# A rational activation's denominator moved from VectorE to ScalarE and Pool, in a fused delta rule and feed-forward kernel

## The chip, the cores and the metric

The kernel runs on one core of a Trainium2 chip. A core has a matrix engine (TensorE; PE in the profile, with its weight loads as PEld), VectorE (DVE), ScalarE (ACT), Pool (GpSimd) and SyncE (SP, which here only issues DMAs). Each engine takes its own instructions in order. The metric is the device time of one execution in microseconds; the median of three runs of the kernel before is 764.67 us (763.59 to 764.72).

## What is computed

A delta-rule attention over 4 batches, 8 heads, 768 steps and a head size of 48 (with the keys divided by their norms), and on its output a feed-forward part with a rational activation:

```python
for t in range(S):
    y[t] = q[t] @ state
    state = state + beta[t] * outer(k[t], v[t] - k[t] @ state)
x = y, heads side by side               # 3072 tokens x 384
h = x @ w_in                            # 3072 x 2048
P = a[0] + a[1]*h + a[2]*h**2 + a[3]*h**3
Q = 1 + abs(b[0])*abs(h) + abs(b[1])*h**2
out = (P / (Q + 1e-6)) @ w_out          # 3072 x 384
```

## The kernel before

Time is cut into 12 chunks of 64 steps. For each chunk the delta rule is solved in matrix form (stages keys, gram, inverse, blocks, solve, next, outputs), with two f16 halves for each operand and so three matmul passes for each product. A chunk yields 256 tokens, all batches side by side. The feed-forward part handles them in 8 units of 256 hidden columns each, 96 units in all. A unit's tile is 128 partitions x 512 (two blocks of 128 hidden columns, 256 tokens each).

One unit n runs through these steps:

- `hidden` (L857): 18 matmuls of 256 columns into `ph`, a PSUM tile of the pool `ps_h` (two buffers).
- `numerator` (L874): ScalarE makes z = |B1 ph| (L884) and u = A3 ph + a2 (L885). VectorE makes w = (z + B0) ph (L888), ScalarE w = |w| (L890). B1, B0, A3 and the like are columns of a small table `msc`, one number for each partition. w, u and z lie in an SBUF tile `mx` with three buffers.
- `cubic` (L892): VectorE multiplies u by ph (L896) and makes (u + A1) ph (L898).
- `quotient` (L900): ScalarE makes ln(w + Q0) (L904) and exp of its negative (L906), the reciprocal of the denominator. VectorE makes the f16 result `mg` (L910), and with two more products the remainder for its lower half (L913, which writes into the next unit's `ph`, and L915). Pool multiplies that remainder by the reciprocal (L917) into the second half of `mg`.
- `accumulate` (L919): 12 matmuls of 384 columns (L931) with both halves into `po`; after the last unit of a chunk the sum is scaled (L948) and stored.

The delta rule's small steps use the same engines: casts on ScalarE (L207, L215), their remainders on VectorE (L217) or Pool (L213), scaling of keys on Pool (L501).

Nothing is scheduled at run time. Every step is a generator that issues a few instructions for each `next`, and a table of numbers, `PLACES`, holds for each step of each chunk or unit its place in the whole program's order; `run` sorts by it and calls them one after the other. That sets the order on every engine, and the tile pools add the waits. By that table the hidden steps of 88 of the 96 units come before the last chunk's tokens are made, before the change and after it.

## Time and profile before

| | before |
|---|---|
| median of three runs | 764.67 us |
| the profiled execution | 765.28 us |
| its span, first to last instruction | 763.6 us |
| VectorE busy | 691.9 us |
| ScalarE busy | 661.1 us |
| TensorE busy | 629.3 us |
| Pool busy | 311.7 us |

The span is what the profile shows; 1.7 us of the execution lie outside it. Busy time of an engine counts the time in which at least one of its instructions is under way, so the durations of neighbours that overlap add up to more than it. Ends of matmuls are modelled. Shares are of the span.

### The profile page before, as it was taken

To read this page: it belongs to the slowest core of one execution; us is meant where nothing else is said; L and a number is where in the kernel's file an instruction comes from. 1 tells how busy PE (TensorE), PEld (TensorE's weight loads), DVE (VectorE), ACT (ScalarE), POOL (GpSimd) and SP (SyncE) were. 2 spreads that over 40 slices of the span, in tenths; PEclk is the share of its full clock that TensorE was granted. 3 is DMA by queue.
4 is the path that set the end of the run, shared out by engine and by line. 5 is a ranking of instruction groups with operands and counts; after the bars stand their busy time and mean duration, and the time that the engine had idled before them with its cause. 6 is when DMAs were issued, how large, how long until landed. Compare 5 with 4: busy or idle time off the path is not lost.

```text
span 763.6 us, 23465 instructions
## 1 busy us (share of the span) xinstructions
PE 629.3 (82%) x9520; PEld 506.6 (66%) x9520; DVE 691.9 (91%) x1288; ACT 661.1 (87%) x1301; POOL 311.7 (41%) x321
## 2 busy tenths in 40 slices
PE   1321455886898999898998999999989999999986
PEld 1221455675677788686776787787778877777753
DVE  6789988867898999898998999999989999999995
ACT  4685998978898999798997999999989996899883
POOL 6742262533344265154342463354542432323222
PEclk9955786999799999899999999999999999999999
DMA  9699999778737675678464777685755832600000
GB/s 215 194 213 196 191 174 149 119 130 129 134 73 124 88 117 98 109 124 127 89 115 81 131 118 119 108 131 87 139 81 103 138 58 36 109 1 23 1 21 22
DMA packets 358412, 84.35 MB, mean 110 GB/s; under 512 B 349856, under 2 KB 352928, under 8 KB 358304
## 3 DMA queue, kind: packets, MB, share of 16 engines
q1 hardware_dynamic: 356128, 81.69, 61.0%
q8 instruction: 75, 1.23, 0.7%
q10 hardware_dynamic: 2176, 1.17, 0.5%
q14 instruction: 33, 0.27, 0.1%
HBM read 34.70 MB, written 13.65 MB: 63 GB/s over the span
## 4 chain that ended last, share of the span: by engine, by line
DVE 32%; ACT 25%; PE 20%; DMA 10%; issue 5%; SPq 3%; POOL 2%; ACTq 0%; DVEq 0%; POOLq 0%
PE ph L864 7%; PE po L931 5%; DVE mx L888 3%; ACT mx L885 3%; DVE ph L913 3%; ACT mx L884 3%; DVE mx L915 3%; DVE mx L896 3%; DVE mg L910 3%; DVE mx L898 3%; ACT kp L815 2%; DVE w_out L311 2%; PE pu L396 2%; ACT mx L904 2%; ACT mx L890 2%
## 5 line engine op out<-in xcount | busy, mean ns | idle before, releaser
L917 POOL TENSOR_TENSOR mg<-mx 128x512 f16<-128x512 f32 x96 | 129.7, 1351 | 277.2 <-DVE mx L915 167.5
L931 PE MATMUL po<-w_out,mg 128*128 128x384 f16 x1152 | 214.5, 329 | 4.3 <-POOL mg L917 2.4
L864 PE MATMUL ph<-xT,w_in 128*128 128x256 f16 x1728 | 205.1, 273 | 10.9 <-DVE mx L915 9.3
L864 PEld LDWEIGHTS <-w_in 128*128 128x128 f16 x1728 | 165.6, 98 | 41.0 <-DVE mx L915 9.3
L931 PEld LDWEIGHTS <-mg 128*128 128x128 f16 x1152 | 109.5, 99 | 65.8 <-POOL mg L917 3.1
L910 DVE SCALAR_TENSOR_TENSOR mg<-mx,msc 128x512 f16<-128x512 f32 x96 | 73.3, 764 | 2.7 <-ACT mx L906 2.6
L884 ACT ACTIVATE mx<-ph,msc 128x512 f32<-128x512 f32 x96 | 65.2, 679 | 12.0 <-PE ph L864 10.1
L913 DVE SCALAR_TENSOR_TENSOR ph<-mx,msc,mg 128x512 f32<-128x512 f32 x96 | 73.7, 768 | 1.5
L885 ACT ACTIVATE mx<-ph,coef,msc 128x512 f32<-128x512 f32 x96 | 74.1, 772 | 0.0
L888 DVE SCALAR_TENSOR_TENSOR mx<-mx,msc,ph 128x512 f32<-128x512 f32 x96 | 70.7, 737 | 1.9 <-issue 1.1
L915 DVE SCALAR_TENSOR_TENSOR mx<-mx,msc,ph 128x512 f32<-128x512 f32 x96 | 71.1, 741 | 1.3
L898 DVE SCALAR_TENSOR_TENSOR mx<-mx,msc,ph 128x512 f32<-128x512 f32 x96 | 70.8, 738 | 0.7
L904 ACT ACTIVATE mx<-mx,msc 128x512 f32<-128x512 f32 x96 | 69.3, 722 | 1.1
L890 ACT ACTIVATE mx<-mx 128x512 f32<-128x512 f32 x96 | 60.3, 628 | 10.7 <-DVE mx L888 10.4
L396 PEld LDWEIGHTS <-kbd 128*128 128x128 f16 x1680 | 57.6, 102 | 16.9 <-DVE sw L328 7.3
L896 DVE TENSOR_TENSOR mx<-ph,mx 128x512 f32<-128x512 f32 x96 | 65.4, 681 | 0.4 <-issue 0.2
L396 PEld LDWEIGHTS <-ebd 128*128 128x128 f16 x1728 | 51.2, 98 | 15.6 <-issue 11.4
L396 PE MATMUL pu<-z,ebd 128*128 128x48 f16 x1728 | 52.0, 186 | 11.4 <-DVE z L217 10.1
L906 ACT ACTIVATE mx<-mx 128x512 f32<-128x512 f32 x96 | 60.1, 628 | 1.1
L396 PEld LDWEIGHTS <-wbd 128*128 128x128 f16 x1152 | 33.2, 98 | 40.4 <-issue 38.7
L213 POOL TENSOR_TENSOR mm<-m,mm 128x512 f16<-128x512 f32 x24 | 31.6, 1328 | 34.4 <-ACT mm L207 28.1
L217 DVE SCALAR_TENSOR_TENSOR z<-pu,zmask,z 128x768 f16<-128x768 f32 x36 | 36.4, 1011 | 5.7 <-ACT z L215 5.7
(196 smaller groups left out, 1194.0 us busy)
## 6 DMA issues: line engine op xcount, KB each, us to landing
wsi<-in_moe_w_in_dram SPq DMA_DIRECT2D x8, 768.0 KB, 6.5
wso<-in_moe_w_out_dram SPq DMA_DIRECT2D x8, 768.0 KB, 6.5
gd<-g SPq DMA_DIRECT2D x24, 256.0 KB, 4.6
mbd<-mm SPq DMA_DIRECT2D x24, 256.0 KB, 5.3
wc<-img SPq DMA_DIRECT2D x24, 256.0 KB, 5.1
...
```

The costliest lines, as they stand in the source:

```text
L396: nc.tensor.matmul(dst[p][:, h], head(bd, lp, p * H + h), head(rt, rp, p * H + h), start=start and n == 0 and h == 0, stop=stop and n == l ...
L864: nc.tensor.matmul(ph[:, i], w_in[:, f2, wp, cc, i * P : (i + 1) * P], x[:, xp, cc], start=k == 0, stop=k == 3 * NCC - 1,)
L884: nc.scalar.activation(z, ph, AF.Abs, scale=B1)
L885: nc.scalar.activation(u, ph, AF.Identity, scale=A3, bias=a2)
L888: nc.vector.scalar_tensor_tensor(out=w, in0=z, scalar=B0, in1=ph, op0=ALU.add, op1=ALU.mult)
L896: nc.vector.tensor_mul(u, ph, u)
L898: nc.vector.scalar_tensor_tensor(out=u, in0=u, scalar=A1, in1=ph, op0=ALU.add, op1=ALU.mult)
L910: nc.vector.scalar_tensor_tensor(out=g[:, 0], in0=u, scalar=A0, in1=r, op0=ALU.add, op1=ALU.mult)
L913: nc.vector.scalar_tensor_tensor(out=t, in0=w, scalar=Q0, in1=g[:, 0], op0=ALU.add, op1=ALU.mult)
L915: nc.vector.scalar_tensor_tensor(out=u, in0=u, scalar=A0, in1=t, op0=ALU.add, op1=ALU.subtract)
L917: nc.gpsimd.tensor_mul(g[:, 1], u, r)
L931: nc.tensor.matmul(po[p], g[:, gp, i, p * P : (p + 1) * P], w_out[:, f2, wp, i], start=f2 == lo and i == 0 and k == 0, stop=f2 == hi - 1 a ...
```

## The change

The denominator |b1| h^2 + |b0| |h| is now made from the absolute value alone. ScalarE makes z = |ph| with the constant scale 1 and w = B1 z + B0, with a column as scale and a column as bias; Pool makes w = w z. VectorE has no step in it. `POOL_UNITS` names the units of a chunk for which this holds: all eight. Three more edits go with it: `numerator` stops after z, so that u has a place of its own; `hidden` stops between its two blocks of nine matmuls; and the norm sums of the weights' tables (two matmul calls) go to the buffers of `ps_h` instead of `ps_f`. The table `PLACES` is new throughout, with 3188 places where there were 2996.

```diff
     def total(src, n, nm, pool=ps_f, tag="a"):
-        pf = pool.tile([P, NPAIR * 512 if pool is ps_f else n], F32, tag=tag, name="pf" + nm)[:, :n]
+        pf = pool.tile([P, NPAIR * 512 if pool is ps_f else TG], F32, tag=tag, name="pf" + nm)[:, :n]
...
+    POOL_UNITS = (0, 1, 2, 3, 4, 5, 6, 7)
...
-        pt = total(io, hi - lo, f"o{lo}", ps_f, "a")
+        pt = total(io, hi - lo, f"o{lo}", ps_h, "h")
...
         ph = ps_h.tile([P, 2, TG], F32, tag="h", name=f"ph_{n}")
+        unit[n] = {"ph": ph}
         for i in range(2):
...
-        unit[n] = {"ph": ph}
+            if i == 0:
+                yield
...
-        nc.scalar.activation(z, ph, AF.Abs, scale=B1)
+        on_pool = f2 in POOL_UNITS
+        nc.scalar.activation(z, ph, AF.Abs, scale=1.0 if on_pool else col(1))
+        yield
+        A3, B1, _, B0, A0, Q0 = (col(i) for i in range(6))
         nc.scalar.activation(u, ph, AF.Identity, scale=A3, bias=a2)
         d.update(u=u, w=w, r=r, A0=A0, Q0=Q0)
         yield
-        nc.vector.scalar_tensor_tensor(out=w, in0=z, scalar=B0, in1=ph, op0=ALU.add, op1=ALU.mult)
-        yield
-        nc.scalar.activation(w, w, AF.Abs)
+        if on_pool:
+            nc.scalar.activation(w, z, AF.Identity, scale=B1, bias=B0)
+            yield
+            nc.gpsimd.tensor_mul(w, w, z)
+        else:
+            nc.vector.scalar_tensor_tensor(out=w, in0=z, scalar=B0, in1=ph, op0=ALU.add, op1=ALU.mult)
+            yield
+            nc.scalar.activation(w, w, AF.Abs)
...
     PLACES = {
         "hidden": (
-            (439,),
+            (395, 436),
...
```

ScalarE's order around unit 29 (the sixth of chunk 3), whose tile is `mx_6136`, in the kernel before, from its absolute value of `ph` to its second absolute value; `mx_6012` and `mx_6248` are the units ahead of and behind it, `z_1` is a step of the delta rule's solve:

```order
L904 ACTIVATE mx_6012<-mx_6012,msc_5451 128x512
L884 ACTIVATE mx_6136<-ph_6117,msc_5451 128x512 [waits PE_49,Pool_49]
L885 ACTIVATE mx_6136<-ph_6117,coef,msc_5451 128x512
L215 ACTIVATE z_1_6191<-pu_6058,zmask 128x768 [waits DVE_49,PE_49,Pool_49]
L906 ACTIVATE mx_6012<-mx_6012 128x512 [waits Activation_49]
L225 ACTIVATE sq_7_6208,fs_6207<-v_6139 128x768 [waits DMAHW7_49,DMAHW0_49]
L890 ACTIVATE mx_6136<-mx_6136 128x512 [waits DVE_49]
L884 ACTIVATE mx_6248<-ph_6229,msc_5451 128x512 [waits PE_49,Pool_49]
```

The same engine and unit now, its tile is `mx_6026`, from the absolute value (L889) over u (L892) and the affine step (L896) to the logarithm (L916); L918 is the exponential, `xT` the tokens' halves, `lgx` a scale's logarithm:

```order
L889 ACTIVATE mx_6026<-ph_5996 128x512 [waits PE_49]
L242 ACTIVATE lgx_6033<-xs_5934 128x1 [waits DVE_49]
L243 ACTIVATE lgx_6033<-lgx_6033,consts 128x1 [waits Activation_49]
L892 ACTIVATE mx_6026<-ph_5996,coef,msc_5343 128x512
L896 ACTIVATE mx_6026<-mx_6026,msc_5343 128x512
L553 COPY wt_92<-bblk 128x16
L215 ACTIVATE xT_5933<-px_6014,sf_5935 128x768 [waits DVE_49,PE_49]
L918 ACTIVATE mx_5931<-mx_5931 128x512
L215 ACTIVATE z_0_6137<-pu_6073,zmask 128x768 [waits PE_49]
L916 ACTIVATE mx_6026<-mx_6026,msc_5343 128x512 [waits Pool_49]
```

Where ScalarE waited for VectorE ahead of the second absolute value, it now waits for Pool ahead of the logarithm, and four instructions of other work lie between the affine step and that wait.

Pool's order in the kernel before, with the remainders' products of units 25 to 27 (`mg_5788`, `mg_6018`, `mg_6055`); `kw` is the scaling of the keys, `kn`, `rr` and `mm` are remainders of the delta rule:

```order
L501 TENSOR_TENSOR kw<-kw,nrm_5650 128x16x48 [waits DMAHW6_49,DMAHW5_49,DMAHW7_49,DMAHW4_49,DVE_49]
L917 TENSOR_TENSOR mg_5788<-mx_5631 128x512 [waits DVE_49,PE_49]
L213 TENSOR_TENSOR rr_5992<-v_3786,rr_5992 128x384 [waits Activation_49]
L917 TENSOR_TENSOR mg_6018<-mx_5717 128x512 [waits DVE_49,PE_49]
L213 TENSOR_TENSOR kn_90<-kw,kn_90 128x2x2x48 [waits Activation_49,Pool_49]
L213 TENSOR_TENSOR kn_90<-kw,kn_90 128x2x2x48
L213 TENSOR_TENSOR rr_5992<-v_3786,rr_5992 128x384
L213 TENSOR_TENSOR mm_6034<-m_6_6027,mm_6034 128x4x2x64 [waits DMAHW1_49,DMAHW0_49,Activation_49]
L213 TENSOR_TENSOR mm_6034<-m_6_6027,mm_6034 128x4x2x64
```

Pool's order now, at the same units: L929 are the remainders' products of units 25 to 27 (`mg_5773`, `mg_5860`, `mg_6029`), L898 with `mx_5931` and `mx_6026` the denominators of units 28 and 29, L502 the scaling of the keys:

```order
L929 TENSOR_TENSOR mg_5773<-mx_5494 128x512 [waits DVE_49,PE_49]
L502 TENSOR_TENSOR kw<-kw,nrm_5478 128x16x48 [waits DMAHW3_49,DMAHW2_49,DMAHW4_49,DMAHW1_49,DVE_49]
L929 TENSOR_TENSOR mg_5860<-mx_5606 128x512 [waits DVE_49,PE_49,Activation_49]
L898 TENSOR_TENSOR mx_5931<-mx_5931 128x512 [waits Activation_49,Pool_49]
L213 TENSOR_TENSOR rr_6009<-v_3920,rr_6009 128x384 [waits Activation_49]
L213 TENSOR_TENSOR kn_90<-kw,kn_90 128x2x2x48 [waits DMAHW6_49,DMAHW5_49,Pool_49]
L213 TENSOR_TENSOR rr_6009<-v_3920,rr_6009 128x384
L898 TENSOR_TENSOR mx_6026<-mx_6026 128x512 [waits Activation_49,Pool_49]
L213 TENSOR_TENSOR kn_90<-kw,kn_90 128x2x2x48
L929 TENSOR_TENSOR mg_6029<-mx_5748 128x512 [waits DVE_49,PE_49]
L213 TENSOR_TENSOR mm_6192<-m_6_6006,mm_6192 128x4x2x64 [waits DMAHW2_49,DMAHW1_49,Activation_49]
```

Two denominators stand between what was there, each behind Pool instructions that wait for other engines.

The last rows of ScalarE in the kernel before, from the second absolute value of unit 94 (`mx_13742`) on; unit 95 is `mx_13775`, L948 the scaling of the result:

```order
L890 ACTIVATE mx_13742<-mx_13742 128x512 [waits DVE_49]
L884 ACTIVATE mx_13775<-ph_13752,msc_13461 128x512 [waits PE_49,Pool_49]
L885 ACTIVATE mx_13775<-ph_13752,coef,msc_13461 128x512
L904 ACTIVATE mx_13742<-mx_13742,msc_13461 128x512 [waits Activation_49]
L906 ACTIVATE mx_13742<-mx_13742 128x512 [waits Activation_49]
L890 ACTIVATE mx_13775<-mx_13775 128x512 [waits DVE_49]
L904 ACTIVATE mx_13775<-mx_13775,msc_13461 128x512 [waits Activation_49]
L906 ACTIVATE mx_13775<-mx_13775 128x512 [waits Activation_49]
L948 ACTIVATE ob_13860<-po_0_0_13612,kp_0_13264 128x384 [waits DMAHW7_49,DMAHW6_49,PE_49]
L948 ACTIVATE ob_13860<-po_0_1_13613,kp_0_13264 128x384 [waits PE_49]
```

The same place now, with units 94 (`mx_13744`) and 95 (`mx_13778`):

```order
L889 ACTIVATE mx_13744<-ph_13725 128x512 [waits PE_49,Pool_49]
L892 ACTIVATE mx_13744<-ph_13725,coef,msc_13477 128x512
L896 ACTIVATE mx_13744<-mx_13744,msc_13477 128x512 [waits Activation_49]
L889 ACTIVATE mx_13778<-ph_13759 128x512 [waits PE_49,Pool_49]
L892 ACTIVATE mx_13778<-ph_13759,coef,msc_13477 128x512
L896 ACTIVATE mx_13778<-mx_13778,msc_13477 128x512 [waits Activation_49]
L916 ACTIVATE mx_13744<-mx_13744,msc_13477 128x512 [waits Pool_49]
L918 ACTIVATE mx_13744<-mx_13744 128x512 [waits Activation_49]
L916 ACTIVATE mx_13778<-mx_13778,msc_13477 128x512 [waits Pool_49]
L918 ACTIVATE mx_13778<-mx_13778 128x512 [waits Activation_49]
L960 ACTIVATE ob_13860<-po_0_0_13616,kp_0_13299 128x384 [waits DMAHW7_49,DMAHW6_49,PE_49]
L960 ACTIVATE ob_13860<-po_0_1_13617,kp_0_13299 128x384 [waits PE_49]
```

ScalarE now makes z, u and w of both units first, and then the logarithms and exponentials, each logarithm behind a wait for Pool.

## Rows read from the trace of the kernel before

**Rows 1.** The page's busy line: busy us of each engine, share of the span, number of instructions.

```profile
PE 629.3 (82%) x9520; PEld 506.6 (66%) x9520; DVE 691.9 (91%) x1288; ACT 661.1 (87%) x1301; POOL 311.7 (41%) x321
```

**Rows 2.** Busy time of each engine in three stretches that make up the span. The columns are the stretch and its length in us, then busy us (instructions) of PE, PEld, DVE, ACT and POOL, the granted TensorE clock, the DMA engines' share and GB/s.

```profile
0.00:180.00 180.00, 86.75 (x1494) 73.30 (x1495) 146.35 (x294) 139.94 (x286) 86.55 (x107) 0.81 0.88 174
180.00:660.00 480.00, 450.06 (x7115) 365.57 (x7114) 451.93 (x845) 439.64 (x864) 195.62 (x192) 0.98 0.64 106
660.00:764.00 104.00, 92.50 (x915) 67.77 (x912) 93.62 (x152) 81.55 (x153) 29.57 (x24) 0.99 0.11 22
```

**Rows 3.** The same view for four shorter stretches.

```profile
420.00:480.00 60.00, 59.08 (x946) 47.93 (x945) 59.06 (x111) 58.35 (x116) 28.20 (x29) 1.00 0.73 122
480.00:540.00 60.00, 58.40 (x945) 47.82 (x943) 58.53 (x108) 58.01 (x114) 27.57 (x27) 1.00 0.66 106
660.00:750.00 90.00, 86.09 (x878) 64.33 (x876) 88.86 (x146) 79.27 (x150) 26.60 (x22) 1.00 0.10 21
750.00:764.00 14.00, 6.40 (x39) 3.44 (x36) 4.76 (x7) 2.28 (x4) 2.97 (x2) 0.96 0.11 29
```

**Rows 4.** Groups of instructions by line and shape: instructions of a unit on VectorE, ScalarE and Pool. After the bar: busy us, mean ns of one, idle us of the engine just before them and what ended most of it.

```profile
L917 POOL TENSOR_TENSOR mg<-mx 128x512 f16<-128x512 f32 x96 | 129.7, 1351 | 277.2 <-DVE mx L915 167.5 <-ACT mx L904 18.4 <-PE pu L396 10.5
...
L885 ACT ACTIVATE mx<-ph,coef,msc 128x512 f32<-128x512 f32 x96 | 74.1, 772 | 0.0
...
L910 DVE SCALAR_TENSOR_TENSOR mg<-mx,msc 128x512 f16<-128x512 f32 x96 | 73.3, 764 | 2.7 <-ACT mx L906 2.6
...
L888 DVE SCALAR_TENSOR_TENSOR mx<-mx,msc,ph 128x512 f32<-128x512 f32 x96 | 70.7, 737 | 1.9 <-issue 1.1 <-ACT mx L885 0.7
L904 ACT ACTIVATE mx<-mx,msc 128x512 f32<-128x512 f32 x96 | 69.3, 722 | 1.1
L896 DVE TENSOR_TENSOR mx<-ph,mx 128x512 f32<-128x512 f32 x96 | 65.4, 681 | 0.4 <-issue 0.2
L884 ACT ACTIVATE mx<-ph,msc 128x512 f32<-128x512 f32 x96 | 65.2, 679 | 12.0 <-PE ph L864 10.1 <-DVE msc L847 0.7 <-DVE mg L910 0.5
L890 ACT ACTIVATE mx<-mx 128x512 f32<-128x512 f32 x96 | 60.3, 628 | 10.7 <-DVE mx L888 10.4
L906 ACT ACTIVATE mx<-mx 128x512 f32<-128x512 f32 x96 | 60.1, 628 | 1.1
```

**Rows 5.** The timeline of one unit near the end, where only the feed-forward part runs: start us, duration us, engine, line and operation; in brackets the idle time before it. L864 is the hidden step, L931 the second matmul.

```profile
740.10 2.14 PE L864 MATMUL ph<-xT,w_in 128*128 128x256 f16 x18
...
742.08 2.11 PE L931 MATMUL po<-w_out,mg 128*128 128x384 f16 x12
...
742.74 0.76 DVE L913 SCALAR_TENSOR_TENSOR ph<-mx,msc,mg 128x512 f32<-128x512 f32 x1
...
743.54 0.75 DVE L915 SCALAR_TENSOR_TENSOR mx<-mx,msc,ph 128x512 f32<-128x512 f32 x1
...
744.20 0.74 DVE L888 SCALAR_TENSOR_TENSOR mx<-mx,msc,ph 128x512 f32<-128x512 f32 x1
...
744.34 2.14 PE L864 MATMUL ph<-xT,w_in 128*128 128x256 f16 x18
744.45 1.28 POOL L917 TENSOR_TENSOR mg<-mx 128x512 f16<-128x512 f32 x1 [2.95 <-ACT mx L904]
744.86 0.68 DVE L896 TENSOR_TENSOR mx<-ph,mx 128x512 f32<-128x512 f32 x1
...
745.46 0.82 DVE L910 SCALAR_TENSOR_TENSOR mg<-mx,msc 128x512 f16<-128x512 f32 x1
746.21 0.73 DVE L898 SCALAR_TENSOR_TENSOR mx<-mx,msc,ph 128x512 f32<-128x512 f32 x1
...
746.98 0.76 DVE L913 SCALAR_TENSOR_TENSOR ph<-mx,msc,mg 128x512 f32<-128x512 f32 x1
```

**Rows 6.** The first view again, for line 888 alone: busy us and number of its instructions in two of the three stretches.

```profile
0.00:180.00 180.00, 2.97 (x4) 0.81 0.88 174
180.00:660.00 480.00, 52.98 (x72) 0.98 0.64 106
```

**Rows 7.** Two groups of casts from PSUM on ScalarE, the first with a column as scale, the second with a constant.

```profile
L215 ACT ACTIVATE z<-pu,zmask 128x768 f16<-128x768 f32 x36 | 32.3, 897 | 7.8 <-PE pu L396 7.8
...
L215 ACT ACTIVATE et<-pe 128x768 f16<-128x768 f32 x12 | 9.7, 805 | 1.7 <-PE pe L396 1.7
```

**Rows 8.** The timeline in the middle of the span: a product on Pool that starts while VectorE is in L910.

```profile
442.23 0.75 DVE L910 SCALAR_TENSOR_TENSOR mg<-mx,msc 128x512 f16<-128x512 f32 x1
...
442.48 1.63 POOL L917 TENSOR_TENSOR mg<-mx 128x512 f16<-128x512 f32 x1 [2.96 <-ACT mx L885]
```

**Rows 9.** Who waited for whom: us in total, times, longest us.

```profile
ACT mx L890 <- DVE mx L888: 10.4, 15, 2.0
...
ACT mx L884 <- PE ph L864: 10.1, 17, 3.2
...
PE ph L864 <- DVE mx L915: 9.3, 13, 2.0
...
ACT z L215 <- PE pu L396: 7.8, 8, 2.6
```

More of the change, by code (lines that the diff above doesn't have):

```diff
@@ L877, in numerator, with col @@
         d = unit[n]
-        A3, B1, A1, B0, A0, Q0 = (toks[c]["m"][:, i, f2 : f2 + 1] for i in range(6))
+        def col(i):
+            return toks[c]["m"][:, i, f2 : f2 + 1]
         ph = d["ph"]
@@ new lines @@
+            (54,),
+            (150,),
+            (524,),
+            (710,),
+            (928,),
+            (1178,),
+            (1420,),
+            (1682,),
+            (1905,),
+            (2173,),
+            (2442,),
+        ),
+        "load_q": (
+            (26,),
+            (147,),
+            (373,),
+            (526,),
+            (655,),
+            (910,),
+            (1210,),
+            (1408,),
+            (1704,),
+            (1889,),
+            (2161,),
+            (2349,),
@@ new lines @@
+        "kbd": (
+            (71,),
+            (288,),
+            (409,),
+            (534,),
+            (724,),
+            (938,),
+            (1244,),
+            (1490,),
+            (1740,),
+            (1945,),
+            (2231,),
+            (2465,),
+        ),
+        "gram": (
+            (72, 89, 90),
+            (294, 306, 314),
+            (437, 438, 440),
+            (558, 572, 573),
+            (757, 775, 806),
+            (972, 1003, 1049),
+            (1245, 1250, 1270),
+            (1499, 1509, 1548),
+            (1751, 1765, 1819),
+            (1965, 1966, 2019),
+            (2254, 2270, 2300),
+            (2479, 2498, 2555),
+        ),
@@ new lines @@
+        "wbd": (
+            (208,),
+            (514,),
+            (653,),
+            (836,),
+            (1146,),
+            (1388,),
+            (1567,),
+            (1826,),
+            (2059,),
+            (2316,),
+            (2600,),
+            (2792,),
+        ),
+        "solve": (
[12 rows of a table added]
+        ),
+        "zero_m": (
+            (297,),
+        ),
+        "zero_q": (
+            (307,),
+        ),
+        "knbd": (
+            (309,),
+            (427,),
+            (747,),
+            (966,),
+            (1214,),
+            (1496,),
+            (1636,),
+            (1927,),
+            (2165,),
+            (2450,),
+            (2607,),
+        ),
@@ L1323 @@
+        "qbd": (
+            (),
+            (383,),
+            (585,),
+            (823,),
+            (1050,),
+            (1297,),
+            (1561,),
+            (1798,),
+            (2040,),
+            (2281,),
+            (2558,),
+            (2734,),
         ),
@@ new lines @@
+            (673, 675),
+            (697, 701),
+            (729, 730),
+            (768, 769),
+            (789, 791),
+            (819, 829),
+            (851, 859),
+            (876, 885),
+            (908, 909),
+            (946, 952),
+            (975, 980),
+            (1013, 1015),
+            (1031, 1032),
+            (1064, 1067),
+            (1082, 1097),
+            (1107, 1110),
+            (1159, 1160),
+            (1182, 1184),
+            (1218, 1219),
+            (1249, 1258),
@@ new lines @@
+            (1272, 1287),
+            (1303, 1308),
+            (1335, 1340),
+            (1356, 1365),
+            (1398, 1404),
+            (1426, 1438),
+            (1457, 1468),
+            (1492, 1493),
+            (1515, 1518),
+            (1536, 1546),
+            (1578, 1593),
+            (1625, 1626),
+            (1634, 1635),
+            (1674, 1685),
+            (1705, 1712),
+            (1741, 1747),
+            (1775, 1790),
+            (1797, 1799),
+            (1832, 1835),
@@ new lines @@
+            (467, 471),
+            (482, 484),
+            (521, 577),
+            (626, 628),
+            (666, 668),
+            (694, 708),
+            (725, 726),
+            (755, 767),
+            (793, 805),
+            (839, 840),
+            (849, 857),
+            (879, 880),
+            (895, 905),
+            (927, 962),
+            (971, 976),
+            (1021, 1022),
+            (1052, 1053),
+            (1061, 1062),
+            (1090, 1091),
+            (1113, 1124),
@@ L1845 @@
+            (3160, 3163, 3164),
+            (3172, 3173, 3177),
+            (3178, 3179, 3180),
+            (3181, 3182, 3185, 3186, 3187),
         ),
```

1353 lines of the change are left out of this document (597 added, 756 removed), and 174 rows, old and new, of the table PLACES.

## The prediction

> **What bounds the kernel now.** I read the page's busy line first, then the busy time by stretch, then the groups by shape, the timeline where only the feed-forward part is left, and the waits. The busy line shows three engines close together: VectorE 691.9 us (91%), ScalarE 661.1 (87%), TensorE 629.3 (82%), and Pool at 311.7 (41%) [rows 1]. An average over the span hides where that binds, so I cut it in three [rows 2]. Up to 180 us no engine is above 82% while the DMA engines are at 0.88: weights are loaded, and the first chunks of the delta rule run one behind the other. From 180 to 660 us, VectorE is busy 451.9 of 480 us (94.2%), TensorE 450.1 (93.8%), ScalarE 439.6 (91.6%): three engines carry nearly the same load, and each waits for the other two. From 420 to 540 us all three are at 97 to 98% [rows 3]. From 660 to 750 us it is VectorE at 88.9 of 90 with TensorE at 86.1; the last 14 us are the drain.
>
> So VectorE leads, but by 2 us over TensorE and 12 us over ScalarE in the stretch that holds most of the work. What VectorE gives up can be cashed only as far as those two let it.
>
> **The change part by part.**
>
> VectorE. One scalar_tensor_tensor of each unit goes (L888, 96 x 737 ns) [rows 4]. Neighbours on VectorE overlap a little, so its place in the queue is the distance from its start to the next start: 744.20 to 744.86, 0.66 us [rows 5]. 96 x 0.66 = 63 us go, VectorE falls to 629 us. Of the 96, 72 lie in the middle stretch [rows 6]: 451.9 - 72 x 0.66 = 404.4 us, 84% of 480. Nothing is added on VectorE, and its waits stay those of the other products.
>
> ScalarE. Each unit has L884 (absolute value of a PSUM tile with a column as its scale, 679 ns) and L890 (absolute value in SBUF, no column, 628) [rows 4]. The first loses its column, the second becomes a step from SBUF with a column as scale and one as bias. What a column costs: L885 has one more than L884 and takes 772 against 679, 93 ns; L904 has one and L906 none, 722 against 628, 94 ns [rows 4]; on 128x768 tiles from PSUM the form with a scale column takes 897 ns and that with a constant 805, 92 ns [rows 7]. So the pair goes from 679 + 628 = 1307 to (679 - 93) + (628 + 2 x 93) = 1400 ns: 93 ns more, 72 x 0.093 = 6.7 us in the middle, 8.9 in all. The affine step from SBUF is not in the trace. Bounds: with the lighter absolute value and only L904's 722 for the step, the pair is 1308 and the price nothing; if the absolute value keeps its 679 and the step takes the 814 of the sum above, it is 1493 and the price 13.4 us in the middle. I take 6.7, since three pairs of rows agree on the column. ScalarE in the middle: 439.6 + 6.7 = 446.3 us. It becomes the fuller of the two engines that the change touches.
>
> Pool. 96 products of 128x512 are added. The same product with an f16 output takes 1351 ns on average [rows 4], so 129.7 us more, 441 in all; in the middle 195.6 + 72 x 1.351 = 293 of 480 us (61%). The f32 output isn't in the trace at this size. A Pool product that starts beside VectorE's L910, which reads two SBUF tiles, took 1.63 us [rows 8], one alone 1.28 [rows 5], while L910 kept its 0.75. The Trainium skill ("GPSIMD Engine Reference", section 8, Key points) says that the two engines share SBUF interfaces and collide when a VectorE instruction has two SBUF inputs; the rows agree and show that it is Pool that pays. By that rule every new product could cost some 0.35 us more, an estimate from those two rows; Pool would stand at about 66% in the middle and the sum would not move.
>
> The new hand-over. Before, ScalarE's second absolute value waited for VectorE's product; now the logarithm (L904, in the new numbering L916) waits for Pool's. Waits of L890 for L888 were 10.4 us in all [rows 9], and go. In their place stands a wait for 1.35 us instead of 0.74. In the order of unit 29, shown with the change, ScalarE has four instructions between its affine step and the logarithm: a 16-column copy, an xT step, an exponential and a z step. From the rows the last two alone are 0.63 + 0.90 us [rows 4, 7], which covers a product that starts at once. It doesn't always: in the piece of Pool's queue shown there, the scaling of the keys and an earlier unit's product stand ahead of a unit's denominator, and all that is queued behind the logarithm on ScalarE then waits too (exponentials of other units, then VectorE's L910 and TensorE's second matmuls). I take the new waits as large as the old, 10 us, between zero and one more wait of 0.3 us in each of 72 units, 22 us.
>
> The rest. TensorE issues the same matmuls; hidden units in two halves let others slip between them, and I cost that at nothing, since in the middle TensorE is already at 93.8%. The two norm sums that use the other banks are four matmuls. The steps' new places I take as doing for the new load what the old ones did for the old. Up to 180 us I leave the time as it is: only 3 or 4 units lie there [rows 6], and neither the loads nor the delta rule's chain change.
>
> The sum. In the middle ScalarE has 446.3 us to do and TensorE 450.1 with its modelled ends. VectorE as the fullest engine got 94.2% there, and ScalarE 97.3% from 420 to 480 us [rows 3]. With VectorE out of the three-way coupling I take 95% on ScalarE: 446.3 / 0.95 = 469.8 us instead of 480, 10.2 less. At the end, VectorE's six steps of a unit take 4.24 us (742.74 to 746.98), and TensorE needs 1.98 us (740.10 to 742.08) and 2.11 us for its two blocks [rows 5]; TensorE takes over as the bound at 4.1 us, 0.15 us less for each of the eight units whose hidden step comes after the last chunk's tokens, 1.2 us. Against it the last unit's chain gets longer by 0.81 + 1.35 - 0.74 - 0.63 = 0.8 us. Net: -10.6 us on the profiled execution's 765.28 (span 763.6 and 1.7 around it), and so from the median 764.67, which lies 0.6 lower, to 754 us.
>
> **The rivals.**
>
> *TensorE is the only bound left.* The stretch from 420 to 540 us shows that TensorE can be kept at 98% [rows 3]. If the finer steps bring the whole middle there, it takes 450.1 / 0.98 = 459.3 us, 20.7 less: 744 us. For it: VectorE's slack and the split of the hidden matmuls. Against it: ScalarE would have to stand at 97.2%.
>
> *No change worth a name.* At 446.3 / 480 = 93.0% on ScalarE, the middle is as long as before: 764 us. ScalarE has 91.6% now; it must gain 1.4 points to break even.
>
> *Slower: ScalarE keeps its gaps.* ScalarE's idle time in the middle is 480 - 439.6 = 40.4 us. If it is set by what ScalarE waits for besides L888 (hidden matmuls, the solve) [rows 9], and Pool's longer product puts back what L888 gave, the middle is 446.3 + 40.4 = 486.7 us, 6.7 more: 771 us. It decides as soon as less than 6.7 of the 40.4 us go; 0.1 us more of waiting for Pool in each unit costs 7.2 us. For it: Pool takes instructions in order and is then 61% busy, and its 1.35 us stand inside each unit's chain. Against it: the logarithms are placed behind other work. The Trainium skill ("GPSIMD Engine Reference", section 4.1, Engine selection) advises against Pool for elementwise work, as about twice slower than VectorE on two inputs. The rows agree, 1351 against 681 ns for the same product [rows 4]; by that rule this is the case to expect.
>
> **How the numbers follow.** 754 us: 0.46, its own range 748 to 760. TensorE-bound, 744: 0.16. No change, 760 to 767: 0.13. Slower, 767 to 780: 0.25. A measurement of this kernel tells about 0.2% (1.5 us) from no change; of the third case I count 0.05 as faster, 0.06 as the same, 0.02 as slower. Faster 0.67, same 0.06, slower 0.27. The range 740 to 773 leaves out the best of the second case and the worst of the last, and takes in the price of ScalarE's step from nothing to 13.4 us.
>
> **What would show it.** In the new profile: VectorE near 629 us, ScalarE near 670, Pool near 441 or more; the absolute value from PSUM near 586 ns, the affine step near 814; from 180 to 660 us ScalarE at about 95%; waits of the logarithm for Pool near 10 us. I am wrong if the affine step takes over 900 ns, if those waits pass 17 us, or if the first 180 us move by more than a few us, for which I have no term.

## The result and the profile after

The changed kernel takes 772.56 us (median of 5 runs, 771.82 to 774.46) against 764.72 us for the kernel before (763.59 to 768.07): ratio 1.0097, 95% interval 1.0069 to 1.0124. It is slower by 7.8 us; 754 us had been forecast.

The busy line of the page after, beside [rows 1]:

```profile
PE 626.0 (81%) x9520; PEld 504.3 (65%) x9520; DVE 687.7 (89%) x1192; ACT 663.1 (86%) x1301; POOL 456.2 (59%) x417
```

VectorE has lost 96 instructions (from 1288 to 1192) and only 4.2 us of busy time, from 691.9 to 687.7; the forecast was 629. Pool has grown by 144.5 us (forecast 129.7) and ScalarE by 2.0 (forecast 8.9).

The same three stretches as [rows 2] (busy time of each engine, then the granted clock, the DMA share and GB/s):

```profile
0.00:180.00 180.00, 85.66 (x1452) 71.76 (x1452) 141.71 (x296) 139.58 (x293) 87.94 (x106) 0.82 0.88 171
180.00:660.00 480.00, 440.79 (x7034) 358.68 (x7034) 453.15 (x760) 435.56 (x849) 301.13 (x263) 1.00 0.61 106
660.00:771.00 111.00, 99.58 (x1042) 73.85 (x1038) 92.82 (x139) 87.96 (x162) 67.14 (x48) 0.99 0.14 27
```

In the middle VectorE is at 94.4%, as before (94.2%), while ScalarE has gone down to 90.7% and TensorE to 91.8%. VectorE is still the fullest engine there, with fewer instructions. So single instructions must have become longer. The groups by shape (mean ns is the last number before the second bar), beside those of [rows 4], show which:

```profile
L922 DVE SCALAR_TENSOR_TENSOR mg<-mx,msc 128x512 f16<-128x512 f32 x96 | 87.1, 907 | 4.4 <-ACT mx L918 4.1
L925 DVE SCALAR_TENSOR_TENSOR ph<-mx,msc,mg 128x512 f32<-128x512 f32 x96 | 84.2, 877 | 4.8
L927 DVE SCALAR_TENSOR_TENSOR mx<-mx,msc,ph 128x512 f32<-128x512 f32 x96 | 71.4, 744 | 2.2
L910 DVE SCALAR_TENSOR_TENSOR mx<-mx,msc,ph 128x512 f32<-128x512 f32 x96 | 70.8, 738 | 1.5
L569 DVE TENSOR_TENSOR pr<-wt,ab 128x16 f32<-128x16 f32 x12 | 10.6, 887 | 0.4
L582 DVE TENSOR_TENSOR pr<-gb,wt 128x64 f32<-128x64 f32 x24 | 9.8, 446 | 0.1
L569 DVE TENSOR_TENSOR pr<-wt,ab 128x4 f32<-128x4 f32 x12 | 7.7, 645 | 0.8
L588 DVE TENSOR_TENSOR pr<-ab,wt 128x64 f32<-128x64 f32 x24 | 7.7, 362 | 0.1
L569 DVE TENSOR_TENSOR pr<-wt,ab 128x36 f32<-128x36 f32 x12 | 7.6, 632 | 0.4
...
L896 ACT ACTIVATE mx<-mx,msc 128x512 f32<-128x512 f32 x96 | 78.0, 812 | 0.0
L889 ACT ACTIVATE mx<-ph 128x512 f32<-128x512 f32 x96 | 56.7, 591 | 8.8 <-PE ph L866 7.5
...
L898 POOL TENSOR_TENSOR mx<-mx 128x512 f32<-128x512 f32 x96 | 128.6, 1339 | 73.5 <-ACT mx L896 66.8
```

L922 is the old L910, L925 the old L913. These are groups of the kernel before that [rows 4] does not hold (the inverse's small products have line numbers lower by one there, L568, L581, L587):

```profile
L913 DVE SCALAR_TENSOR_TENSOR ph<-mx,msc,mg 128x512 f32<-128x512 f32 x96 | 73.7, 768 | 1.5
L915 DVE SCALAR_TENSOR_TENSOR mx<-mx,msc,ph 128x512 f32<-128x512 f32 x96 | 71.1, 741 | 1.3
...
L587 DVE TENSOR_TENSOR pr<-ab,wt 128x64 f32<-128x64 f32 x24 | 5.3, 261 | 0.0
L581 DVE TENSOR_TENSOR pr<-gb,wt 128x64 f32<-128x64 f32 x24 | 4.2, 219 | 0.0
L568 DVE TENSOR_TENSOR pr<-wt,ab 128x36 f32<-128x36 f32 x12 | 2.9, 246 | 0.4
L568 DVE TENSOR_TENSOR pr<-wt,ab 128x16 f32<-128x16 f32 x12 | 2.1, 176 | 0.4
L568 DVE TENSOR_TENSOR pr<-wt,ab 128x4 f32<-128x4 f32 x12 | 2.0, 165 | 0.6
```

The 96 products that went were worth 70.7 us of durations. Of that 51 us come back on the others: L922 96 x (907 - 764) = 13.7, L925 96 x (877 - 768) = 10.5, the three shapes of L569 12 x (711 + 480 + 386) = 18.9, L582 24 x 227 = 5.4, L588 24 x 101 = 2.4. All of these read both inputs from SBUF. L910 and L927, of the same length and type but with one input in PSUM (`ph`), stay at 738 and 744 ns.

The timeline of the changed kernel shows how they get longer (start, duration):

```profile
498.07 1.27 POOL L929 TENSOR_TENSOR mg<-mx 128x512 f16<-128x512 f32 x1
...
498.34 1.02 DVE L569 TENSOR_TENSOR pr<-wt,ab 128x16 f32<-128x16 f32 x1
...
499.61 0.20 DVE L569 TENSOR_TENSOR pr<-wt,ab 128x36 f32<-128x36 f32 x1
...
499.99 1.28 POOL L898 TENSOR_TENSOR mx<-mx 128x512 f32<-128x512 f32 x1 [0.66 <-ACT mx L896]
500.10 1.72 DVE L922 SCALAR_TENSOR_TENSOR mg<-mx,msc 128x512 f16<-128x512 f32 x1
...
522.39 0.68 DVE L582 TENSOR_TENSOR pr<-gb,wt 128x512 f32<-128x512 f32 x1
...
522.61 1.60 POOL L898 TENSOR_TENSOR mx<-mx 128x512 f32<-128x512 f32 x1 [0.38 <-ACT mx L896]
```

The 16-column L569 starts 0.27 us after Pool's L929 and ends at 499.36, 0.02 us after Pool does; the 36-column one, with Pool idle, takes 0.20. L922 starts with 1.17 us of Pool's new product left and takes 1.72. At 522 us it is the other way round: VectorE's L582 starts first and keeps its 0.68, and the new product takes 1.60 in place of 1.28, as in [rows 8]. So whoever starts second waits for the other to finish. Counted over all records of the trace ("beside": a Pool instruction has started before and still has over 0.1 us to go):

| VectorE's instruction, both inputs in SBUF unless said | no such Pool instruction | beside the new product L898 | of Pool left, mean |
|---|---|---|---|
| L922 | 0.767 us (60) | 1.251 (14) | 0.69 |
| L925 | 0.772 (61) | 1.106 (19) | 0.54 |
| L910, one input in PSUM | 0.736 (30) | 0.738 (28) | 0.74 |
| L927, one input in PSUM | 0.744 (53) | 0.745 (18) | 1.06 |

From some 0.25 us left on, a 128x512 product that comes second takes what is left of Pool's instruction and 0.55 us more (0.45 left: 1.00; 0.79: 1.34; 1.12: 1.68). With all of Pool's instructions counted, 36 of the L922 and 35 of the L925 start beside one. In the trace of before 29 of the L910 did, but near its end (0.25 us left on average: mean 0.811 us against 0.744 alone), and 3 of the L913: there the order kept them nearly apart. The Trainium skill ("SBUF — State Buffer", section Who interferes with whom) states this rule: a VectorE instruction with two SBUF inputs contends with a Pool instruction that reads SBUF, not with one that only writes; one with at most one SBUF input, outside the modes that use two ports, does not; and what they share is an exclusive lock, for which the order of issue decides who blocks. The trace agrees: two SBUF inputs go from 0.77 to 1.25 and 1.11 us, one keeps its 0.74; that Pool's pure writes do not block is seen in run 3.

The waits (total, times, longest), beside [rows 9]:

```profile
PE ph L866 <- DVE mx L927: 15.4, 19, 1.5
...
ACT mx L889 <- PE ph L866: 7.5, 11, 1.9
...
ACT mx L916 <- POOL mx L898: 5.0, 10, 1.4
```

The new wait, the logarithm for Pool's product, is 5.0 us in all, less than the 10 that were forecast. TensorE's wait for VectorE has grown from 9.3 to 15.4. In sum VectorE is busy for 4.2 us less and idle for 11.4 us more (83.1 against 71.7), which gives a span longer by 7.2 us.

### The profile page after: what moved, and what is told of

Read it like the earlier page. It is cut to its first block, busy times and chain, and to the rows that moved or that the text cites. A ratio compares the mean times of both kernels' runs of the same rounds, so it can differ in the third digit from the quotient of the medians.

```text
span 770.8 us, 23546 instructions
## 1 busy us (share of the span) xinstructions
PE 626.0 (81%) x9520; PEld 504.3 (65%) x9520; DVE 687.7 (89%) x1192; ACT 663.1 (86%) x1301; POOL 456.2 (59%) x417
## 3 DMA queue, kind: packets, MB, share of 16 engines
q10 hardware_dynamic: 2176, 1.17, 0.5%
## 4 chain that ended last, share of the span: by engine, by line
DVE 33%; PE 22%; ACT 20%; DMA 9%; issue 7%; POOL 4%; SPq 4%; ACTq 0%; DVEq 0%; POOLq 0%
PE ph L866 8%; PE po L943 5%; DVE mg L922 4%; DVE ph L925 4%; DVE mx L910 3%; ACT mx L892 3%; DVE mx L908 3%; DVE pr L569 3%; DVE mx L927 3%; ACT mx L896 2%; DVE z L217 2%; DMA kbd<-tk 2%; ACT mx L889 2%; PE pu L397 2%; ACT mx L916 2%
## 5 line engine op out<-in xcount | busy, mean ns | idle before, releaser
L866 PE MATMUL ph<-xT,w_in 128*128 128x256 f16 x1728 | 210.1, 274 | 18.6 <-DVE mx L927 15.4
L943 PE MATMUL po<-w_out,mg 128*128 128x384 f16 x1152 | 213.9, 328 | 10.5 <-DVE mg L922 6.8
L929 POOL TENSOR_TENSOR mg<-mx 128x512 f16<-128x512 f32 x96 | 136.6, 1425 | 114.1 <-DVE mx L927 80.2
L898 POOL TENSOR_TENSOR mx<-mx 128x512 f32<-128x512 f32 x96 | 128.6, 1339 | 73.5 <-ACT mx L896 66.8
L943 PEld LDWEIGHTS <-mg 128*128 128x128 f16 x1152 | 108.7, 98 | 72.3 <-DVE mg L922 10.1
L922 DVE SCALAR_TENSOR_TENSOR mg<-mx,msc 128x512 f16<-128x512 f32 x96 | 87.1, 907 | 4.4 <-ACT mx L918 4.1
L925 DVE SCALAR_TENSOR_TENSOR ph<-mx,msc,mg 128x512 f32<-128x512 f32 x96 | 84.2, 877 | 4.8
L896 ACT ACTIVATE mx<-mx,msc 128x512 f32<-128x512 f32 x96 | 78.0, 812 | 0.0
L892 ACT ACTIVATE mx<-ph,coef,msc 128x512 f32<-128x512 f32 x96 | 74.4, 775 | 1.0 <-DVE msc L848 0.7
L916 ACT ACTIVATE mx<-mx,msc 128x512 f32<-128x512 f32 x96 | 69.1, 719 | 5.3 <-POOL mx L898 5.0
L927 DVE SCALAR_TENSOR_TENSOR mx<-mx,msc,ph 128x512 f32<-128x512 f32 x96 | 71.4, 744 | 2.2
L910 DVE SCALAR_TENSOR_TENSOR mx<-mx,msc,ph 128x512 f32<-128x512 f32 x96 | 70.8, 738 | 1.5
L889 ACT ACTIVATE mx<-ph 128x512 f32<-128x512 f32 x96 | 56.7, 591 | 8.8 <-PE ph L866 7.5
L918 ACT ACTIVATE mx<-mx 128x512 f32<-128x512 f32 x96 | 60.1, 627 | 0.7
L307 POOL TENSOR_SCALAR w_out<-w_out 128x768 f32<-128x768 f32 x15 | 16.6, 1109 | 41.7 <-ACT w_out L305 39.1
```

What stands on the lines that cost most here:

```text
L866: nc.tensor.matmul(ph[:, i], w_in[:, f2, wp, cc, i * P : (i + 1) * P], x[:, xp, cc], start=k == 0, stop=k == 3 * NCC - 1,)
L892: nc.scalar.activation(u, ph, AF.Identity, scale=A3, bias=a2)
L896: nc.scalar.activation(w, z, AF.Identity, scale=B1, bias=B0)
L898: nc.gpsimd.tensor_mul(w, w, z)
L910: nc.vector.scalar_tensor_tensor(out=u, in0=u, scalar=A1, in1=ph, op0=ALU.add, op1=ALU.mult)
L922: nc.vector.scalar_tensor_tensor(out=g[:, 0], in0=u, scalar=A0, in1=r, op0=ALU.add, op1=ALU.mult)
```

## Experiments

Two theories stand against each other. *The shared read* (also called the port): Pool's 96 added products, and new places that put VectorE's two-input instructions beside Pool's, make VectorE stand still, so that what L888 gave comes back. *The hand-over*: the logarithm, and what is queued behind it, waits for a product of 1.34 us in place of 0.74. A third theory, *the order*, has the new places cost the 8 us by themselves; a fourth, *Pool's time*, that Pool is late for its other work because its queue is fuller (runs 9 and 10). The ratios are to runs of the kernel before on the same chip (medians 764.1 to 765.1 us).

### 1. The new places with VectorE's old step in seven units of eight

```diff
-    POOL_UNITS = (0, 1, 2, 3, 4, 5, 6, 7)
+    POOL_UNITS = (0,)
```

> The changed kernel in its new order, with the denominators of seven of eight units made the old way again (VectorE's step and ScalarE's second absolute value; only unit 0 of each chunk stays on Pool). Theory 'shared port' (a VectorE instruction with two SBUF inputs that starts while Pool is at work waits for Pool's end): with 84 Pool products gone, L922 falls from 907 to about 780 ns, Pool to about 330 us; VectorE stays near 690 us since its own step is back; the time lies near the kernel before, 762 to 770 us. Theory 'order' (the new places alone cost the 8 us): 772 us or more, since the order stays and the old load doesn't fit it. Theory 'hand-over' (Pool's latency ahead of the logarithm): waits of the logarithm for Pool go from 5 us to under 1, the time falls by about as much, to 767.

Measured: 872.76 us, ratio 1.1417 (1.1378 to 1.1456). (By the table of places, VectorE's step of four units comes after the neighbouring unit's remainder has been written into their `ph`, so their w holds other values; the amount of work is the same.)

```profile
ACT mx L902 <- DVE mx L900: 45.7, 27, 5.5
ACT mx L889 <- PE ph L866: 43.3, 30, 6.2
DVE mx L900 <- ACT mx L892: 39.3, 20, 5.2
```

This is far outside what the shared read and the hand-over allowed, and no answer on the cause. The order's "772 us or more" takes it in, but its 8 us do not: the old step, put where the new ones stand, makes ScalarE and VectorE wait for each other by turns. An order made for one set of instructions can't be used to weigh another.

### 2. The new steps in the old places

The edit keeps ScalarE's affine step and Pool's product and takes the table of places, the undivided `hidden` step and the banks of the norm sums from the kernel before.

```diff
-        nc.scalar.activation(z, ph, AF.Abs, scale=B1)
+        nc.scalar.activation(z, ph, AF.Abs)
...
-        nc.vector.scalar_tensor_tensor(out=w, in0=z, scalar=B0, in1=ph, op0=ALU.add, op1=ALU.mult)
-        yield
-        nc.scalar.activation(w, w, AF.Abs)
+        nc.scalar.activation(w, z, AF.Identity, scale=B1, bias=B0)
+        yield
+        nc.gpsimd.tensor_mul(w, w, z)
```

> The kernel before, in its old order, with the new steps in the places of the old ones (ScalarE's affine step where VectorE's step was, Pool's product where ScalarE's second absolute value was). Theory 'shared port': the old order wasn't made for a busy Pool either; L910 rises from 764 to over 880 ns, VectorE's busy time falls by less than 20 us instead of 63, and the time is 768 to 785 us. Theory 'order': 755 to 762 us, since the old places were good and the load is less. Theory 'hand-over': the logarithm, placed right behind the product in many units, waits for Pool for 30 us or more, and the time is over 780.

Measured: 842.72 us, ratio 1.1010 (1.0979 to 1.1040). Its waits, and the group of one VectorE product:

```profile
ACT mx L904 <- POOL mx L890: 47.0, 33, 5.7
```

```profile
L910 DVE SCALAR_TENSOR_TENSOR mg<-mx,msc 128x512 f16<-128x512 f32 x96 | 96.4, 1004 | 18.6 <-ACT mx L906 18.3
```

In the old places the hand-over is real and large: the logarithm waits 47 us for Pool. The new places take that down to 5. VectorE's L910 is longer still, 1004 ns, and VectorE's busy time, 695.4 us, is above that of before although its 96 products are gone. Both parts of what was expected came true for the hand-over; of the shared read, VectorE's part came true and the time lies far above its 768 to 785 us. The order's 755 to 762 us did not come.

### 3. Pool's product replaced by fills

The first fill goes to a spare tile, the second over w, so that the denominators are a constant.

```diff
+    idle = cpool.tile([P, 384], F32, name="idle")
...
-            nc.gpsimd.tensor_mul(w, w, z)
+            nc.gpsimd.memset(idle, 0.5)
+            nc.gpsimd.memset(m[:, 1:3].rearrange("p a b t -> p (a b t)"), 0.5)
```

> The changed kernel, with Pool's denominator product replaced by two memsets of 384 and 1024 columns, the second over w: Pool is kept as long, the logarithm waits for it as before, but Pool reads nothing. The product w z is left out, so the denominators are a constant. Theory 'shared port': VectorE's two-input instructions no longer meet a reading Pool in half of the cases; L922 falls from 907 to about 780 ns, L925 from 877 to about 780, VectorE's busy time from 688 to 630 to 645 us, the time to 752 to 762 us. Theory 'hand-over' and theory 'order': VectorE may change but the time stays at 768 to 774, since Pool's time in the chain and the places are the same.

Measured: 758.55 us, ratio 0.9918 (0.9888 to 0.9948). The busy line of the page, the logarithm's wait, and from the timeline a VectorE product that starts beside a fill of Pool:

```profile
PE 627.2 (83%) x9520; PEld 505.3 (67%) x9520; DVE 671.1 (89%) x1192; ACT 662.2 (88%) x1301; POOL 445.4 (59%) x513
```

```profile
ACT mx L918 <- POOL mx L900: 2.9, 5, 1.1
```

```profile
406.43 0.95 POOL L900 MEMSET mx<- 128x1024 f32 x1 [1.84 <-ACT mx L897]
...
407.00 0.74 DVE L924 SCALAR_TENSOR_TENSOR mg<-mx,msc 128x512 f16<-128x512 f32 x1
```

Pool is busy almost as long as in the change (10.8 us less) and the logarithm still waits for it (2.9 us), but the time falls by 14.0 us and VectorE's busy time by 16.6. L924 (the change's L922) started beside a fill 13 times, mean 0.73 us; beside Pool's f16 product L931, 11 times, mean 1.20. Of the 14 us the difference of the waits, some 2 us, can be the hand-over's; the rest goes with Pool's reading, since Pool's time is 2% less only. The time is in the shared read's range; VectorE, at 671.1, is above its 630 to 645.

### 4. No step of Pool or VectorE at all

The denominator can be had on ScalarE alone as a completed square: with |b1|z^2 + |b0|z = (sqrt|b1| z + |b0| / (2 sqrt|b1|))^2 - b0^2 / (4|b1|), where z is |h|, the constant goes into Q0. This needs b1 other than zero. The places are the change's.

```diff
...
-            nc.scalar.activation(w, z, AF.Identity, scale=B1, bias=B0)
+            nc.scalar.activation(w, z, AF.Square, scale=B1, bias=B0)
             yield
-            nc.gpsimd.tensor_mul(w, w, z)
```

Left out here are the edits that put the new constants into the tables of columns.

> The changed kernel and its order, with the square completed: w = (sqrt(B1) z + B0 / (2 sqrt(B1)))^2 by ScalarE's Square with a column as scale and one as bias, the constant b0^2 / (4 b1) taken off Q0 in the table; no product on Pool and none on VectorE. Theory 'shared port': this is what the prediction took the change for, VectorE 625 to 640 us, ScalarE near 665, Pool near 320, L922 near 765 ns, and the time is near the forecast, 750 to 758 us. Theory 'order': 766 us or more. Theory 'hand-over': the waits for Pool go, 5 us, so 765 to 768.

Measured: 749.47 us (747.98 to 750.33), ratio 0.9792 (0.9765 to 0.9819): faster than both kernels. Busy line, middle stretch and three groups:

```profile
PE 624.5 (83%) x9520; PEld 505.7 (68%) x9520; DVE 661.4 (88%) x1195; ACT 659.8 (88%) x1304; POOL 323.2 (43%) x321
```

```profile
180.00:660.00 480.00, 459.54 (x7331) 374.25 (x7330) 447.09 (x789) 451.31 (x886) 212.32 (x200) 1.00 0.62 107
```

```profile
L929 DVE SCALAR_TENSOR_TENSOR mg<-mx,msc 128x512 f16<-128x512 f32 x96 | 78.6, 819 | 5.4 <-ACT mx L925 5.2
L932 DVE SCALAR_TENSOR_TENSOR ph<-mx,msc,mg 128x512 f32<-128x512 f32 x96 | 77.0, 802 | 2.2
...
L577 DVE TENSOR_TENSOR pr<-wt,ab 128x16 f32<-128x16 f32 x12 | 8.2, 682 | 0.4
```

ScalarE has as much to do as in the change; Pool's product is gone. That is worth 23.1 us (21.7 against run 7, which has the same tables). The order's 766 us or more and the hand-over's 765 to 768 did not come. In the middle ScalarE is now at 94.0%, near the 95% of the forecast. The shared read has two misses in size: the time is 0.5 us under its 750 to 758, and VectorE, expected at 625 to 640, is still 32 us above the forecast's 629, because its two-input instructions meet Pool's other work (L929 819 ns against 764 before).

### 5. The square in the old places

The same square, with the places, hidden steps and banks of the kernel before.

> ScalarE's Square as in e4_square_on_scalar, but in the kernel before and its old order: the Square stands where VectorE's step stood, the old second absolute value is empty. The same amounts of work as e4 in the places of before. Theory 'shared port' leaves open how the old places fit; the two-input instructions of the small inverse (L568, 176 to 246 ns in before) should stay near that, since the same Pool work lies beside them, and VectorE's busy time should fall by nearly the whole 63 us, to 630 to 640. If places don't matter once Pool has no denominators: 745 to 755 us. If the old places misfit ScalarE's new row, as in e2 (843), 765 or more.

Measured: 763.25 us, ratio 0.9981 (0.9960 to 1.0002). Waits, the f16 product (before: L910), and one of the inverse's products:

```profile
ACT mx L892 <- PE ph L872: 19.8, 23, 3.8
DVE mg L917 <- ACT mx L913: 14.8, 20, 2.7
```

```profile
L917 DVE SCALAR_TENSOR_TENSOR mg<-mx,msc 128x512 f16<-128x512 f32 x96 | 86.1, 897 | 14.9 <-ACT mx L913 14.8
...
L576 DVE TENSOR_TENSOR pr<-wt,ab 128x16 f32<-128x16 f32 x12 | 2.1, 175 | 0.4
```

VectorE's busy time falls to 648.7 us, lower than in any other run, and the time by 1.6 us, with no change inside the interval: the freed time turns into waits for TensorE and ScalarE (10.1 and 2.6 us before). None of the expected ranges took in the time, and VectorE is 9 us above its 630 to 640. 12.8 us of VectorE are lost on L917: without L888, and with the same work on Pool, it starts beside a running Pool instruction 37 times with 0.57 us left on average, where L910 did 29 times with 0.25. So the old places kept them nearly apart only for the old load. The new places are worth about 14 us at the lighter load (763.25 to 749.47), though in them the small instructions of the inverse collide: 4 of its 108 products start beside a reading Pool instruction here and 35 in run 4, and the 16-column one takes 175 ns here and 682 there.

### 6 and 7. Half of the products, and all

Run 4 with Pool's square w*w after ScalarE's affine step, in the units 0, 2, 4, 6 of each chunk (run 6) or in all (run 7); the edit is shown against the change.

```diff
...
-            nc.scalar.activation(w, z, AF.Identity, scale=B1, bias=B0)
+            nc.scalar.activation(w, z, AF.Identity if f2 in BY_POOL else AF.Square, scale=B1, bias=B0)
             yield
-            nc.gpsimd.tensor_mul(w, w, z)
+            if f2 in BY_POOL:
+                nc.gpsimd.tensor_mul(w, w, w)
```

> e4_square_on_scalar with the square made on Pool in every second unit (ScalarE does the affine step with the same two columns, Pool multiplies w by itself): 48 Pool products of 128x512 more, ScalarE's work the same, places the same. Theory 'shared port': a dose half way between e4 (749.5 us, VectorE 661) and the change (772.6, VectorE 688): VectorE 672 to 678, L922's counterpart 850 to 880 ns, 757 to 764 us. Theory 'hand-over': the time follows the waits of the logarithm for Pool, which are 5 us in the change, so it rises by under 3 us, to 752.

> The same with the square on Pool in all units: the change's load and places with e4's tables. Both theories: as the change, VectorE 685 to 692, Pool near 455, 769 to 776 us. If it were nearer to e4, the gain of e4 would come from the tables or the logarithm's argument and not from Pool's products.

Measured: 758.60 us, ratio 0.9908 (0.9873 to 0.9944), and 771.12 us, ratio 1.0076 (1.0046 to 1.0105). Busy line of run 6, then of run 7:

```profile
PE 628.3 (83%) x9520; PEld 505.7 (67%) x9520; DVE 675.3 (89%) x1195; ACT 660.4 (87%) x1304; POOL 374.9 (49%) x369
```

```profile
PE 629.5 (82%) x9520; PEld 507.1 (66%) x9520; DVE 687.8 (89%) x1195; ACT 661.1 (86%) x1304; POOL 427.8 (56%) x417
```

None, 48 and 96 products give 749.5, 758.6 and 771.1 us, and VectorE 661.4, 675.3 and 687.8 us: some 0.23 us of time and 0.28 us of VectorE for each product, on an engine that executes none of them. ScalarE stays within 1.3 us. Both runs came as the shared read had it, but for Pool's 428 us in run 7 (near 455 expected); the hand-over allowed run 6 no more than 752. Run 7 is nearly as slow as the change, with another formula.

### 8. Pool's product in two halves

```diff
-            nc.gpsimd.tensor_mul(w, w, z)
+            for i in range(2):
+                nc.gpsimd.tensor_mul(w[:, i], w[:, i], z[:, i])
```

> The changed kernel with each of Pool's denominator products issued as two of 256 columns. The same reading in all, Pool some 20 to 40 us busier. Theory 'shared port', with the port held from an instruction's start to its end: VectorE gets in between the halves, so the longest waits behind a denominator are some 0.8 us instead of 1.3; L922 falls from 907 to 850 to 880 ns, VectorE by 5 to 15 us, and the time by 0 to 6 us although Pool has more to do. Theory 'hand-over': the logarithm's data come later by 0.3 to 0.4 us, and the time rises by 5 us or more, to 778.

Measured: 767.25 us (762.32 to 769.79, 10 runs), ratio 1.0024 (0.9998 to 1.0050). Its waits and busy line:

```profile
ACT mx L917 <- POOL mx L899: 8.7, 17, 1.6
```

```profile
PE 631.5 (82%) x9520; PEld 508.0 (66%) x9520; DVE 680.6 (89%) x1192; ACT 663.5 (86%) x1301; POOL 476.1 (62%) x513
```

Pool works 20 us longer and the logarithm waits longer, and yet the median is 5.3 us below that of the change, with VectorE 7.1 us lower: VectorE waits behind a half rather than a whole product. Its L923 (the change's L922) starts beside a half 18 times with 0.41 us left on average and takes 0.96 us, where L922 had 0.69 left and took 1.25. The hand-over alone would have made this run slower (778 expected).

### 9 and 10. Pool's work with nobody waiting for it

Run 4 again, with work on Pool that the result does not need: in run 9 two products of 256 columns that read w, in run 10 a 16-column product that reads w and three fills.

```diff
...
+            for i in range(2):
+                nc.gpsimd.tensor_mul(idle[:, 0:TG], w[:, i], w[:, i])
```

```diff
...
+            nc.gpsimd.tensor_mul(idle[:, 0:16], w[:, 0, 0:16], w[:, 0, 0:16])
+            for n0 in (0, 0, 128):
+                nc.gpsimd.memset(idle[:, n0:], 0.5)
```

> The kernel of e4_square_on_scalar (749.5 us, VectorE 661.4 us, Pool 323.2), and for each unit two products of 256 columns on Pool besides, which read w after ScalarE's square and write into a spare tile that nobody reads. Nothing waits for them; they do no work that the result needs. Some 1.3 to 1.4 us of Pool for each unit, about as much as in the change. Theory of the shared read (a two-input VectorE instruction stands still while Pool reads SBUF): VectorE's busy time rises by 12 to 20 us as with the change's product, and the time to 758 to 765 us, though there is no hand-over at all. Theory of the hand-over (what costs in the change is that the logarithm waits for Pool): no consumer, so 749 to 752 us and VectorE within 3 us of 661.

> The same kernel, with a 16-column product that reads w and then three fills (384, 384 and 256 columns) of the spare tile on Pool for each unit in place of the two products: about the same time of Pool, but nearly all of it only writes. Again nothing waits for it. Theory of the shared read: VectorE within 5 us of 661 and 749 to 754 us. Theory of Pool's time (Pool is late for its own work, the f16 remainders and the scaled keys, because its queue is fuller): both this run and the one with reads take the same, some 755 to 760 us. Hand-over theory: 749 to 752 us, as with the reads.

Measured: 761.62 us, ratio 0.9965 (0.9941 to 0.9989), and 755.97 us, ratio 0.9894 (0.9866 to 0.9923). Busy line of run 9, then of run 10 with one of its groups:

```profile
PE 625.8 (82%) x9520; PEld 504.5 (66%) x9520; DVE 680.9 (90%) x1195; ACT 659.9 (87%) x1304; POOL 455.1 (60%) x513
```

```profile
PE 626.8 (83%) x9520; PEld 505.5 (67%) x9520; DVE 670.1 (89%) x1195; ACT 660.0 (88%) x1304; POOL 461.5 (61%) x705
```

```profile
L936 DVE SCALAR_TENSOR_TENSOR ph<-mx,msc,mg 128x512 f32<-128x512 f32 x96 | 81.3, 847 | 2.2
```

With nothing waiting, reading products cost 12.1 us, so the hand-over can't be the whole cause; that is what the shared read expected. Run 10 missed its bound for VectorE (within 5 us of 661; it is 8.7 above) and lies 6.5 us above run 4, where the shared read allowed 4.5. That time is what Pool's time expected, but it expected the same for run 9, which takes 5.7 us more, with VectorE 10.8 us busier. In run 10's trace two-input instructions that start beside the fills keep their length (13 of L933, mean 0.740 us). But Pool's own work comes at other moments: 10 of L936 stand beside Pool's f16 product L940, mean 1.076, where in run 4 it was 4 of L932, mean 0.848. Of the inverse's 108 products 42 start beside a reading Pool instruction, 35 in run 4. L936 (847 ns against 802) and the inverse's products make up VectorE's additional time. So more time of Pool, even if it only writes, costs something, here by shifting when Pool reads.

Together with the change, run 3 and run 8 this gives a table:

| Pool's added work | nobody waits | the logarithm waits |
|---|---|---|
| none (run 4) | 749.5 us, VectorE 661.4 | |
| mostly fills (runs 10, 3) | 756.0, 670.1 | 758.6, 671.1 |
| products that read, in halves (runs 9, 8) | 761.6, 680.9 | 767.3, 680.6 |
| products that read, whole (the change) | | 772.6, 687.7 |

The waiting costs 2.6 us where Pool writes and 5.6 where it reads in halves, with VectorE as busy as without it; these are no more than the logarithm's waits themselves, 2.9 and 8.7 us. (Run 8's products have two tensors as inputs and run 9's one, so that Pool is 21 us busier in run 8.) The whole products, rather than halves, cost another 5.3 us although the wait is shorter. The profiled span less VectorE's busy time is 79 to 88 us in every kernel with the new places but the first (run 4 86.7, run 10 84.0, run 3 83.6, run 9 79.0, run 6 82.7, run 7 82.3, run 8 87.5, the change 83.1): to within these 8 us the time of these kernels goes with VectorE's busy time, which spreads over 26.

## Why the prediction was wrong

- *The step that failed* is the one on collisions under Pool: that "it is Pool that pays", so that Pool would stand at about 66% "and the sum would not move". It was read off one row pair, in which VectorE had started first [rows 8]. When Pool starts first, VectorE pays. With that the term of VectorE falls: 629 us were predicted, 687.7 measured. Of the difference of 58.7, 26.3 go with Pool's new product (the change against run 4), 12.7 with the new places and what was edited along with them (run 4 against run 5), and 19.7 are there with neither (run 5), 12.8 of these on its L917.
- *VectorE's 96 places of 0.66 us*, 63 us in all: the 96 instructions did go, but even without a product on Pool they gave back no more than 43.2 us of VectorE (run 5), mostly because L917 then meets Pool's reads. That VectorE would be out of the coupling did not follow, since it stays at 94.4% in the middle, where 84% was predicted.
- *"The steps' new places I take as doing for the new load what the old ones did for the old"* was right about the waits (5.0 us for the logarithm against 47 in the old places, run 2) and wrong about VectorE: under the new load neither table keeps its two-input instructions off Pool's reads (907 ns for the f16 product, 1004 in run 2). VectorE is idle 83.1 us in the span against 71.7 before, and the difference lies outside the middle: 38.3 against 33.7 us up to 180 us, and 18.0 against 10.0 after 660. Run 4 has this too (38.2 and 15.6), so it goes with the new places and not with Pool's product; where it comes from was not followed up.
- *ScalarE's terms* held: the absolute value takes 591 ns (586 predicted), the affine step 812 (814). The pair is 96 ns longer, as predicted (93). The durations of all of ScalarE's instructions add up to 8.7 us more (764.8 to 773.5), but its neighbours overlap by 6.7 us more (103.7 to 110.4), so that the busy time rose by 2.0 us and not by 8.9.
- *The hand-over's wait* of 10 us, between 0 and 22, measured 5.0. It lay inside the range and is not the main cause: where it could be set apart, waiting cost 2.6 and 5.6 us (runs 3 and 8), Pool's reading without a wait 12.1 (run 9), of which 6.5 are there with fills too (run 10).
- *The sum without the failed term*: run 4 has nearly the same load on ScalarE, the same 96 instructions less on VectorE and no new product on Pool. It takes 749.5 us, 15.6 less than before, where 10.6 less was forecast. That ScalarE comes to 94.0% in the middle there, near the predicted 95%, is in part luck: VectorE's slack was the reason given, and VectorE is at 93.1%, not 84%.
- *The rivals.* "Slower, 771" names the time, by another way: it had ScalarE keep its gaps because Pool's product comes late for the logarithm. The gaps did stay, ScalarE's idle time in the middle is 44.4 us (40.4 before), but the logarithm's wait for Pool is 5.0 us in the whole span; by the runs it is VectorE, held up by Pool's reads, that is late. Nor was Pool's slowness in itself the main reason, by which the prediction weighed the rule against elementwise work on Pool (1339 against 681 ns for a product now, 1351 against 681 there): the fills of run 3 keep Pool almost as busy, and that run is faster than before. "TensorE the only bound, 744" and "no change, 764" did not come.

What was not tried: places that keep VectorE's two-input instructions off Pool's products, and one of the two inputs in PSUM for L922 and L925.
